# Keys and values in one transfer per block, queries in two per batch, with the heads on the same partitions

## The chip, the core and the metric

The kernel runs on one core of a Trainium2 chip. The metric is device time in microseconds (us), from the first to the last instruction of that core. The core has a matrix engine (TensorE, PE in the profile), whose weight loads are listed apart (PEld), three engines for elementwise work (VectorE, DVE; ScalarE, ACT; GpSimd, POOL) and SyncE (SP), which here only issues transfers. Transfers between the main memory and the core's own memory of 128 partitions run on 16 transfer engines; an engine that issues one spends time of its instruction queue on it (SPq, ACTq, POOLq in the profile). Engines run on their own and wait for each other by semaphores.

## The reference

A retention layer (attention with a fixed decay per head instead of a softmax), then a layer of experts with one expert for each token.

```python
# q, k, v: (8, 8, 576, 64) float32: batch, heads, positions, width of a head
scores = (1 / np.sqrt(64)) * (q @ k.transpose(0, 1, 3, 2))
gamma = 1.0 - 2.0 ** (-5.0 - np.arange(H))
ret = scores * np.where(rel >= 0, gamma[:, None, None] ** rel, 0.0)   # rel = position of q - position of k
x = (ret @ v) as rows of 4608 tokens x 512
probs = softmax(x @ w_gate)                       # 8 experts
out[token] = probs[its best expert] * (relu(x[token] @ w1[e]) @ w2[e])   # e: its best expert
```

## The kernel before

The 576 positions of a batch are cut into four blocks of 128 (`c` = 0 to 3) and a last one of 64 (`c` = 4): 40 blocks in all, numbered `i`. The decay is split into a factor on the keys (`kg`) and one on the queries (`qg`), so that the scores of a block need a triangular mask alone; what lies before the block comes in through a running state (`se`). Keys of a block are loaded (`kt`), scaled on GpSimd (`kk`), transposed on TensorE (`psk`), copied by ScalarE (`kT`), and multiplied with the transposed queries (`pssc`); VectorE masks the scores (`sc`), TensorE multiplies them with the values (`psx`), VectorE copies the result (`xT`), and it goes, transposed back (`psr`, `xr`), to rows of tokens in main memory (`x_rows`), from which the experts' stage gathers its tokens.

```python
P, B, H, S, DH = 128, 8, 8, 576, 64
NP, NCH, REM, NCOL = H // 2, 4, 64, 5
# ... `after(ins, dep)` lets `ins` go only when `dep` is done; ldk has 7 buffers per tag, ldq 2 ...
    def load_q(b, p, dep=None):

        if p == 0:
            qts[b] = ldq.tile([P, H, NCH, DH], F32, tag="q", name="qt")
        h = 2 * p
        after(nc.sync.dma_start(out=qts[b][:, h:h + 2, :, :],
                                in_=q[b, h:h + 2, 0:NCH * P, :].rearrange("h (p s) d -> p h s d", p=P)), dep)


    def load_kv(store, tag, src, i, part, dep):
        b, c = blocks[i]
        if i not in store:
            store[i] = ldk.tile([P, H, DH], F32, tag=tag, name=tag + "t")
        t = store[i]
        hs = slice(part * NP, (part + 1) * NP)
        for u in range(part + 1):
            ps = slice(0, P) if part == 0 else slice(u * REM, (u + 1) * REM)
            t0 = c * P + ((1 - u) * REM if part else 0)
            n = P if part == 0 else REM
            after(nc.sync.dma_start(out=t[ps, hs, :], in_=src[b, hs, t0:t0 + n, :].rearrange("h p d -> p h d")), dep)

    def load_k(i, part=None, dep=None):

        if i >= NB:
            return
        b, c = blocks[i]
        for u in range(2) if part is None else (part,):
            if c < NCH:
                load_kv(kts, "k", k, i, u, dep)
                continue
            if i not in kts:
                kts[i] = ldk.tile([P, H, DH], F32, tag="k", name="kt")
            after(nc.sync.dma_start(out=kts[i][u * REM:(u + 1) * REM, :, :],
                                    in_=(q, k)[u][b, :, NCH * P:S, :].rearrange("h p d -> p h d")), dep)

    def load_v(i, part=None, dep=None):

        if i >= NB:
            return
        b, c = blocks[i]
        for u in range(2) if part is None else (part,):
            if c < NCH:
                load_kv(vts, "v", v, i, u, dep)
                continue
            if i not in vts:
                vts[i] = ldk.tile([P, H, DH], F32, tag="v", name="vt")
            after(nc.sync.dma_start(out=vts[i][u * REM:(u + 1) * REM, 0:NP, :],
                                    in_=v[b, u * NP:(u + 1) * NP, NCH * P:S, :].rearrange("h p d -> p h d")), dep)

    load_k(0)
    for p in range(NP):
        load_q(0, p)
    load_v(0)
    load_k(1)
    load_v(1)
    load_q(1, 0)
    for i in range(2, 5):
        load_k(i)
        load_v(i)
        load_q(1, i - 1)
    # ... factors kg, qg; for heads 4 to 7 of a full block kg is made for the swapped halves ...
        mask = attc.tile([P, NP, P], F32, name="mask")
        nc.gpsimd.memset(mask[:, :, :], 0.0)
        for p in range(NP):
            e_ = (p // 2) * REM
            o_ = REM - e_
            nc.gpsimd.tensor_copy(out=mask[e_:e_ + REM, p, 0:REM], in_=tri[e_:e_ + REM, :])
            nc.gpsimd.memset(mask[e_:e_ + REM, p, REM:P], 1.0)
            nc.gpsimd.tensor_copy(out=mask[o_:o_ + REM, p, REM:P], in_=tri[o_:o_ + REM, :])
        return tri, mask
    # ...
    def scale_k(i):
        if i >= NB:
            return
        kk = wk3.tile([P, H, DH], F32, tag="kk")
        nc.gpsimd.tensor_tensor(out=kk[:, :, :], in0=kts.pop(i)[:, :, :],
                                in1=kg[:, blocks[i][1], :].unsqueeze(2).to_broadcast([P, H, DH]), op=ALU.mult)
        kks[i] = kk

    def stage_TK(i):
        if i >= NB:
            return
        kk = kks[i]
        pst = psw.tile([P, 512], F32, tag="W", name="psk")
        for p in range(NP):
            tr(pst[:, p * P:(p + 1) * P], kk[:, 2 * p:2 * p + 2, :].rearrange("p h d -> p (h d)"), ident[:, :])
        kT = wkp.tile([P, NP, P], F32, tag="kT")
        mark["kT"] = nc.scalar.copy(out=kT[:, :, :].rearrange("p a t -> p (a t)"), in_=pst[:, :])
        kTs[i] = kT

    def stage_SC(i):
        if i >= NB:
            return
        b, c = blocks[i]
        kT = kTs.pop(i)
        sc = wkp.tile([P, 2, NP, P], F32, tag="sc")
        scs[i] = sc
        if c < NCH:
            qT = qTs[b]
            for p in (0, 2, 1, 3):
                for o in range(2):
                    u = (p // 2) ^ o
                    for j in range(2):
                        r = slice(j * DH, (j + 1) * DH)
                        mm(pssc[u * DH:(u + 1) * DH, j, p * P + o * DH:(p + 1) * P], kT[r, p, u * DH:(u + 1) * DH],
                           qT[r, p, c * P + o * DH:(c + 1) * P], True, True)
            mark["sc"] = nc.vector.tensor_tensor(
                out=sc[:, :, :, :].rearrange("p j a i -> p j (a i)"), in0=pssc[:, :, :],
                in1=mask[:, :, :].rearrange("p a i -> p (a i)").unsqueeze(1).to_broadcast([P, 2, NP * P]),
                op=ALU.mult)
    # ... else: the last block of 64 ...
```

A matmul of the scores uses 64 of the 128 rows and 64 of the 128 columns of the array: `r` chooses the rows (head `j` of a pair), `u` the columns. Keys of the first half of a block are multiplied with all 128 queries, those of the second half with the last 64 only. Heads 0 to 3 have the first half of the keys on partitions 0 to 63; heads 4 to 7 have it on partitions 64 to 127, which is why `load_kv` loads those heads in two pieces.

The main loop, with what paces the loads (`mark`):

```python
    for i, (b, c) in enumerate(blocks):
        mark.clear()
        if i == 1:
            make_routing()
        if c < NP and b + 1 < B:
            scale_q(b + 1, c)
        scale_k(i + 3)
        stage_SC(i + 1)
        load_k(i + 6, 0, mark.get("sc"))
        stage_TK(i + 2)
        load_k(i + 6, 1, mark.get("kT"))
        stage_S(i + 1)
        load_v(i + 6, 0, mark.get("se"))
        if rf is not None:
            steps(rf, 0.6)
        if i > 0:
            stage_R(i - 1)
        if c == 0 and b > 0:
            stage_L1(b - 1)
        stage_AV(i)
        load_v(i + 6, 1, mark.get("xT"))
        if c < NP and b + 2 < B:
            load_q(b + 2, c, mark.get("xT"))
        if c < NP and b + 1 < B:
            stage_TQ(b + 1, c)
        if c == 0 and b > 0:
            stage_L2(b - 1)
        for (e, j), m in zip(early.get(i, ()), ("sc", "kT", "xT")):
            load_w(e, j, 4, wpool, mark.get(m))
        if (b, c) == (B // 2, 1):
            rf = route_first()
        if rf is not None:
            steps(rf, 0.8)
```

`stage_R` sends the rows of a full block to `x_rows` in one transfer and those of a last block in two, both issued by SyncE. Weights of the first four experts come in 32 pieces: one each in blocks 12, 16, 20, 24 and 28, three each in the last seven blocks (33 to 39), and the other six after the loop. GpSimd issues them.

Of the kernel before, what the change touches and what calls it, by code (L numbers as in the profile page):

```python
# [11 lines left out]
ALU = mybir.AluOpType  # L12
# [29 lines left out]
def kernel(  # L42
# [55 lines left out]
    def load_q(b, p, dep=None):  # L98

        if p == 0:  # L100
            qts[b] = ldq.tile([P, H, NCH, DH], F32, tag="q", name="qt")
        h = 2 * p
        after(nc.sync.dma_start(out=qts[b][:, h:h + 2, :, :],  # L103
                                in_=q[b, h:h + 2, 0:NCH * P, :].rearrange("h (p s) d -> p h s d", p=P)), dep)


    def load_kv(store, tag, src, i, part, dep):
        b, c = blocks[i]
        if i not in store:
            store[i] = ldk.tile([P, H, DH], F32, tag=tag, name=tag + "t")  # L110
        t = store[i]
        hs = slice(part * NP, (part + 1) * NP)
        for u in range(part + 1):
            ps = slice(0, P) if part == 0 else slice(u * REM, (u + 1) * REM)
            t0 = c * P + ((1 - u) * REM if part else 0)
            n = P if part == 0 else REM
            after(nc.sync.dma_start(out=t[ps, hs, :], in_=src[b, hs, t0:t0 + n, :].rearrange("h p d -> p h d")), dep)  # L117

    def load_k(i, part=None, dep=None):
# [4 lines left out]
        for u in range(2) if part is None else (part,):  # L124
            if c < NCH:
                load_kv(kts, "k", k, i, u, dep)
                continue
            if i not in kts:
                kts[i] = ldk.tile([P, H, DH], F32, tag="k", name="kt")
# [3 lines left out]
    def load_v(i, part=None, dep=None):  # L133
# [4 lines left out]
        for u in range(2) if part is None else (part,):  # L138
            if c < NCH:
                load_kv(vts, "v", v, i, u, dep)  # L140
                continue
            if i not in vts:
                vts[i] = ldk.tile([P, H, DH], F32, tag="v", name="vt")
# [4 lines left out]
    for p in range(NP):  # L148
        load_q(0, p)
# [3 lines left out]
    load_q(1, 0)  # L153
    for i in range(2, 5):
        load_k(i)
        load_v(i)
        load_q(1, i - 1)
# [9 lines left out]
    tok = attc.tile([P, 3, NCOL], F32, name="tok")  # L167
# [4 lines left out]
    for u in range(2):  # L172
# [531 lines left out]
    for i, (b, c) in enumerate(blocks):  # L704
# [20 lines left out]
        if c < NP and b + 2 < B:  # L725
            load_q(b + 2, c, mark.get("xT"))
# [242 lines left out]
```

## Time and profile before

| | before |
|---|---|
| time, median of 3 runs | 422.88 us (415.46 to 425.97) |
| span of the profiled run, granted TensorE clock | 422.9 us, 0.943 |
| busy: PE, PEld | 349.8 us (83%), 246.7 us (58%) |
| busy: DVE, ACT, POOL | 159.6 us (38%), 130.1 us (31%), 196.8 us (47%) |
| transfers issued by SyncE | 97152 packets, 33.08 MB, 32.5% of 16 engines' span |
| transfers issued by GpSimd | 18176 packets, 31.47 MB, 34.2% |
| chain that ended last | PE 58%, DMA 18%, SPq 10%, POOL 4%, others |

How to read it: the busy share is the time in which an engine has an instruction of its own under way; issuing a transfer and waiting do not count, so SyncE has no busy time at all here although its queue may be full. The chain that ended last is followed back from the last instruction, at each step to what released it: its shares say on what the end hung, engine by engine. In the attention stage, to about 240 us, one sees keys (`kt`), the queue that issues them (SPq) and TensorE in that chain; after that, TensorE and the weights. L numbers are lines of the kernel: L117 loads keys and values, L103 queries, L271 scales keys, L329 masks scores, L60 and L63 are the helpers that record all matmuls and transposes.

### The profile page before, as it was taken

How to read it: one execution, taken by the hardware profiler on the slowest of the kernel's cores; microseconds unless marked ns; L12 is line 12 of the kernel's file. 1: busy time of each engine (PE TensorE's matmuls, PEld its weight loads, DVE VectorE, ACT ScalarE, POOL GpSimd, SP SyncE). 2: the span in 40 equal slices, each digit the busy share in tenths (PEclk: the TensorE clock that was granted, in tenths of full speed). 3: DMA queues.
4: the chain of work that ended last, by engine and by line, in shares of the span. 5: the costliest groups of instructions: out<-in, count | busy, mean ns of one | idle time of the engine just before them, and what ended most of it. 6: DMA issues, size and time to landing. Idle time of an engine off the chain costs nothing.

```text
span 422.9 us, 11389 instructions
## 1 busy us (share of the span) xinstructions
PE 349.8 (83%) x4626; PEld 246.7 (58%) x4642; DVE 159.6 (38%) x360; ACT 130.1 (31%) x292; POOL 196.8 (47%) x244
## 2 busy tenths in 40 slices
PE   3698986987988878958896659968999999999970
PEld 2486765865866657646675446735555656565630
DVE  3142423341433575714475359512223333232320
ACT  3233442233242432321431222223333332323320
POOL 5752332332424433336764543765656654455320
PEclk9998998898999989969899969989999999999995
DMA  6746665576677767488799999989578822223120
GB/s 174 172 95 141 160 163 150 139 161 166 159 170 166 172 144 184 117 202 208 180 191 189 205 208 230 207 195 192 131 174 189 196 98 98 88 90 112 68 76 22
DMA packets 115389, 65.37 MB, mean 155 GB/s; under 512 B 86142, under 2 KB 107646, under 8 KB 115328
## 3 DMA queue, kind: packets, MB, share of 16 engines
q0 software_dynamic: 18176, 31.47, 34.2%
q1 hardware_dynamic: 97152, 33.08, 32.5%
q8 instruction: 39, 0.64, 0.6%
q14 instruction: 22, 0.18, 0.1%
HBM read 67.14 MB, written 15.20 MB: 195 GB/s over the span
## 4 chain that ended last, share of the span: by engine, by line
PE 58%; DMA 18%; SPq 10%; POOL 4%; issue 3%; DVE 2%; ACT 1%; another core or an unknown queue 1%; POOLq 0%; ACTq 0%
PE py L60 16%; PE pm L60 16%; DMA kt<-in_k_dram 12%; PE psx L60 7%; SPq L117 5%; DMA w2b<-in_moe_w_dram 4%; PE psk L63 4%; POOL kk L271 3%; PE pssc L60 3%; PE pss L60 3%; PE psr L63 3%; PE psq L63 2%; PE pt L63 2%; PE psl L60 1%; SPq L103 1%
## 5 line engine op out<-in xcount | busy, mean ns | idle before, releaser
L271 POOL TENSOR_TENSOR kk<-kt,kg 128x512 f32<-128x512 f32 x40 | 41.9, 1047 | 119.9 <-DMA kt<-in_k_dram 100.0
L794 ACT ACTIVATE ht<-pm 128x384 bf16<-128x384 f32 (+1 forms) x96 | 50.4, 526 | 106.7 <-PE pm L60 98.2
L60 PE MATMUL pm<-xt,w1b 128*128 128x256 bf16 (+1 forms) x512 | 74.6, 305 | 5.6 <-DVE xt L778 5.1
L60 PE MATMUL py<-w2b,ht 128*128 128x512 bf16 x304 | 71.1, 386 | 4.0 <-ACT ht L794 2.5
L809 POOL DMA_INDIRECT out_dram<-ys,tids x40 | 40.8, 1020 | 64.7 <-DVE ys L808 57.9
L60 PEld LDWEIGHTS <-w1b 128*128 128x128 bf16 x512 | 51.0, 100 | 28.6 <-issue 5.9
L63 PE MATMUL psk<-ident,kk 128*128 128x128 f32 x160 | 28.8, 307 | 38.7 <-POOL kk L271 38.6
L60 PEld LDWEIGHTS <-ht 128*128 128x128 bf16 x320 | 30.9, 99 | 39.1 <-issue 3.4
L329 DVE TENSOR_TENSOR sc<-pssc,mask 128x1024 f32<-128x1024 f32 x32 | 39.1, 1221 | 27.0 <-PE pssc L60 14.1
L808 DVE TENSOR_SCALAR ys<-py,gat 128x512 f32<-128x512 f32 x40 | 30.0, 750 | 50.8 <-PE py L60 48.8
L369 DVE COPY xT<-psx 128x512 f32<-128x512 f32 x32 | 22.1, 691 | 66.1 <-PE psx L60 61.1
L648 POOL DMA_INDIRECT xg<-x_rows,tidg x40 | 41.0, 1026 | 11.9 <-issue 9.3
L293 ACT COPY kT<-psk 128x512 f32<-128x512 f32 x40 | 23.4, 586 | 72.9 <-PE psk L63 72.5
L63 PEld LDWEIGHTS psk<-ident,kk 128*128 128x128 f32 x160 | 18.3, 150 | 43.9 <-POOL kk L271 41.7
L60 PE MATMUL psx<-sc,vt 128*64 128x128 f32 (+1 forms) x640 | 39.6, 273 | 0.0
L778 DVE COPY xt<-pt 128x512 bf16<-128x512 bf16 x40 | 15.8, 421 | 54.4 <-PE pt L63 49.4
L261 POOL TENSOR_TENSOR qq<-qt,qg 128x512 f32<-128x512 f32 x32 | 34.0, 1063 | 1.3 <-DMA qt<-in_q_dram 1.1
L60 PEld LDWEIGHTS psx<-sc,vt 128*64 128x64 f32 (+1 forms) x640 | 30.6, 138 | 6.1 <-issue 5.5
L60 PE MATMUL pssc<-qT,kT 64*64 64x128 f32 (+1 forms) x1024 | 32.2, 257 | 1.2 <-issue 0.8
L60 PEld LDWEIGHTS pssc<-qT,kT 64*64 64x64 f32 x1024 | 25.5, 138 | 8.1 <-issue 5.0
L283 ACT COPY qT<-psq 128x512 f32<-128x512 f32 x32 | 19.2, 600 | 32.2 <-PE psq L63 32.2
L310 ACT COPY se<-pss 128x256 f32<-128x256 f32 x32 | 11.9, 372 | 46.5 <-PE psx L60 36.8
(119 smaller groups left out, 361.9 us busy)
## 6 DMA issues: line engine op xcount, KB each, us to landing
qt<-in_q_dram SPq DMA_DIRECT2D x32, 256.0 KB
kt<-in_k_dram SPq DMA_DIRECT2D x40, 128.0 KB
vt<-in_v_dram SPq DMA_DIRECT2D x80, 64.0 KB
kt<-in_k_dram SPq DMA_DIRECT2D x64, 64.0 KB
vt<-in_v_dram SPq DMA_DIRECT2D x32, 128.0 KB
x_rows<-xr SPq DMA_DIRECT2D x32, 128.0 KB
w1b<-in_moe_w_dram POOLq DMA_DIRECT2D x16, 256.0 KB
w2b<-in_moe_w_dram POOLq DMA_DIRECT2D x16, 256.0 KB
```

What stands on the lines that cost most here:

```text
L60: nc.tensor.matmul(out=out, lhsT=lhsT, rhs=rhs, start=start, stop=stop, skip_group_check=True)
L63: nc.tensor.transpose(out=out, in_=in_, identity=identity)
L117: after(nc.sync.dma_start(out=t[ps, hs, :], in_=src[b, hs, t0:t0 + n, :].rearrange("h p d -> p h d")), dep)
L261: nc.gpsimd.tensor_tensor(out=qq[:, :, :].rearrange("p s (h d) -> p h s d", d=DH), in0=qts[b][:, h0:h0 + 2, :, :], in1=qg[:, 0:NCH, h0:h0 ...
L271: nc.gpsimd.tensor_tensor(out=kk[:, :, :], in0=kts.pop(i)[:, :, :], in1=kg[:, blocks[i][1], :].unsqueeze(2).to_broadcast([P, H, DH]), op=A ...
L293: mark["kT"] = nc.scalar.copy(out=kT[:, :, :].rearrange("p a t -> p (a t)"), in_=pst[:, :])
L329: mark["sc"] = nc.vector.tensor_tensor(out=sc[:, :, :, :].rearrange("p j a i -> p j (a i)"), in0=pssc[:, :, :], in1=mask[:, :, :].rearrang ...
L369: mark["xT"] = nc.vector.tensor_copy(out=xTs[b][:, c, :].rearrange("p (w t) -> p w t", w=2), in_=psx[:, :, 0:2 * P])
L648: nc.gpsimd.indirect_dma_start(out=xg[:, :], out_offset=None, in_=x_rows[0:nr, :], in_offset=bass.IndirectOffsetOnAxis(ap=slots[ph][1][:, ...
L794: nc.scalar.activation(out=ht[:, f0:f0 + per, :], in_=pm[:, :, :], func=AF.Relu)
L808: nc.vector.tensor_scalar(out=ys[:, :], in0=py[:, :], scalar1=gat[:, i:i + 1], scalar2=None, op0=ALU.mult)
L809: nc.gpsimd.indirect_dma_start(out=next(outs)[:, :], out_offset=bass.IndirectOffsetOnAxis(ap=tids[:, i:i + 1], axis=0), in_=ys[:, :], in_o ...
```

## The change

Keys and values of a full block come in one transfer each, all eight heads with their positions on the same partitions, instead of three each; the swapped halves of heads 4 to 7 are given up, and with them the third set of decay factors, the two kinds of mask and the order of the score matmuls that went with them. Queries come in two transfers of four heads per batch instead of four of two heads; those of the first batch are issued by ScalarE while SyncE issues keys and values. The pace marks are spread anew. It is for fewer issues: each transfer costs its issuing queue some time, whatever its size.

```diff
--- before.py
+++ after.py
@@ -95,66 +95,57 @@
     NB = len(blocks)
     qts, kts, vts, qrs = {}, {}, {}, {}
 
-    def load_q(b, p, dep=None):
-
-        if p == 0:
+    def load_q(b, g, dep=None, eng=None):
+
+        if g == 0:
             qts[b] = ldq.tile([P, H, NCH, DH], F32, tag="q", name="qt")
-        h = 2 * p
-        after(nc.sync.dma_start(out=qts[b][:, h:h + 2, :, :],
-                                in_=q[b, h:h + 2, 0:NCH * P, :].rearrange("h (p s) d -> p h s d", p=P)), dep)
-
-
-    def load_kv(store, tag, src, i, part, dep):
+        hs = slice(g * NP, (g + 1) * NP)
+        after((eng or nc.sync).dma_start(out=qts[b][:, hs, :, :],
+                                         in_=q[b, hs, 0:NCH * P, :].rearrange("h (p s) d -> p h s d", p=P)), dep)
+
+    def load_kv(store, tag, src, i, dep):
         b, c = blocks[i]
-        if i not in store:
-            store[i] = ldk.tile([P, H, DH], F32, tag=tag, name=tag + "t")
-        t = store[i]
-        hs = slice(part * NP, (part + 1) * NP)
-        for u in range(part + 1):
-            ps = slice(0, P) if part == 0 else slice(u * REM, (u + 1) * REM)
-            t0 = c * P + ((1 - u) * REM if part else 0)
-            n = P if part == 0 else REM
-            after(nc.sync.dma_start(out=t[ps, hs, :], in_=src[b, hs, t0:t0 + n, :].rearrange("h p d -> p h d")), dep)
-
-    def load_k(i, part=None, dep=None):
+        store[i] = ldk.tile([P, H, DH], F32, tag=tag, name=tag + "t")
+        after(nc.sync.dma_start(out=store[i][:, :, :],
+                                in_=src[b, :, c * P:(c + 1) * P, :].rearrange("h p d -> p h d")), dep)
+
+    def load_k(i, dep=None):
 
         if i >= NB:
             return
         b, c = blocks[i]
-        for u in range(2) if part is None else (part,):
-            if c < NCH:
-                load_kv(kts, "k", k, i, u, dep)
-                continue
-            if i not in kts:
-                kts[i] = ldk.tile([P, H, DH], F32, tag="k", name="kt")
+        if c < NCH:
+            load_kv(kts, "k", k, i, dep)
+            return
+        kts[i] = ldk.tile([P, H, DH], F32, tag="k", name="kt")
+        for u in range(2):
             after(nc.sync.dma_start(out=kts[i][u * REM:(u + 1) * REM, :, :],
                                     in_=(q, k)[u][b, :, NCH * P:S, :].rearrange("h p d -> p h d")), dep)
 
... load_v likewise: one transfer for a full block, two for the last block ...
     load_k(0)
-    for p in range(NP):
-        load_q(0, p)
+    load_q(0, 0, eng=nc.scalar)
+    load_q(0, 1, eng=nc.scalar)
     load_v(0)
     load_k(1)
     load_v(1)
-    load_q(1, 0)
     for i in range(2, 5):
         load_k(i)
         load_v(i)
-        load_q(1, i - 1)
+        if i < 4:
+            load_q(1, i - 2)
 
 
     lns = []
... tok, kx: the third set of decay factors goes ...
     kg = attc.tile([P, NCOL, H], F32, name="kg")
     qg = attc.tile([P, NCOL, H], F32, name="qg")
-    for j in range(2):
-        hs = slice(j * NP, (j + 1) * NP)
-        nc.vector.tensor_tensor(out=kg[:, :, hs].rearrange("p c h -> p h c"), in0=kx[:, 2 * j, 0, hs, :],
-                                in1=kx[:, 2 * j, 1, hs, :], op=ALU.mult)
+    nc.vector.tensor_tensor(out=kg[:, :, :].rearrange("p c h -> p h c"), in0=kx[:, 0, 0, :, :],
+                            in1=kx[:, 0, 1, :, :], op=ALU.mult)
     nc.vector.scalar_tensor_tensor(out=qg[:, :, :].rearrange("p c h -> p h c"), in0=kx[:, 1, 0, :, :],
                                    scalar=scale, in1=kx[:, 1, 1, :, :], op0=ALU.mult, op1=ALU.mult)
     nc.vector.tensor_copy(out=kg[0:REM, NCH, :], in_=qg[0:REM, NCH, :])
@@ -211,11 +196,9 @@
         mask = attc.tile([P, NP, P], F32, name="mask")
         nc.gpsimd.memset(mask[:, :, :], 0.0)
         for p in range(NP):
-            e_ = (p // 2) * REM
-            o_ = REM - e_
-            nc.gpsimd.tensor_copy(out=mask[e_:e_ + REM, p, 0:REM], in_=tri[e_:e_ + REM, :])
-            nc.gpsimd.memset(mask[e_:e_ + REM, p, REM:P], 1.0)
-            nc.gpsimd.tensor_copy(out=mask[o_:o_ + REM, p, REM:P], in_=tri[o_:o_ + REM, :])
+            nc.gpsimd.tensor_copy(out=mask[0:REM, p, 0:REM], in_=tri[0:REM, :])
+            nc.gpsimd.memset(mask[0:REM, p, REM:P], 1.0)
+            nc.gpsimd.tensor_copy(out=mask[REM:P, p, REM:P], in_=tri[REM:P, :])
         return tri, mask
 
 
@@ -319,13 +302,12 @@
         scs[i] = sc
         if c < NCH:
             qT = qTs[b]
-            for p in (0, 2, 1, 3):
-                for o in range(2):
-                    u = (p // 2) ^ o
+            for p in range(NP):
+                for u in range(2):
                     for j in range(2):
                         r = slice(j * DH, (j + 1) * DH)
-                        mm(pssc[u * DH:(u + 1) * DH, j, p * P + o * DH:(p + 1) * P], kT[r, p, u * DH:(u + 1) * DH],
-                           qT[r, p, c * P + o * DH:(c + 1) * P], True, True)
+                        mm(pssc[u * DH:(u + 1) * DH, j, p * P + u * DH:(p + 1) * P], kT[r, p, u * DH:(u + 1) * DH],
+                           qT[r, p, c * P + u * DH:(c + 1) * P], True, True)
             mark["sc"] = nc.vector.tensor_tensor(
                 out=sc[:, :, :, :].rearrange("p j a i -> p j (a i)"), in0=pssc[:, :, :],
                 in1=mask[:, :, :].rearrange("p a i -> p (a i)").unsqueeze(1).to_broadcast([P, 2, NP * P]),
@@ -702,18 +684,17 @@
         early[i] = [rest.pop(0) for _ in range(3)]
     rf = None
     for i, (b, c) in enumerate(blocks):
-        mark.clear()
         if i == 1:
             make_routing()
         if c < NP and b + 1 < B:
             scale_q(b + 1, c)
         scale_k(i + 3)
         stage_SC(i + 1)
-        load_k(i + 6, 0, mark.get("sc"))
+        load_k(i + 6, mark.get("sc"))
         stage_TK(i + 2)
-        load_k(i + 6, 1, mark.get("kT"))
         stage_S(i + 1)
-        load_v(i + 6, 0, mark.get("se"))
+        if c in (1, 3) and b + 2 < B:
+            load_q(b + 2, c // 2, mark.get("kT"))
         if rf is not None:
             steps(rf, 0.6)
         if i > 0:
@@ -721,9 +702,7 @@
         if c == 0 and b > 0:
             stage_L1(b - 1)
         stage_AV(i)
-        load_v(i + 6, 1, mark.get("xT"))
-        if c < NP and b + 2 < B:
-            load_q(b + 2, c, mark.get("xT"))
+        load_v(i + 6, mark.get("xT"))
         if c < NP and b + 1 < B:
             stage_TQ(b + 1, c)
         if c == 0 and b > 0:
```

## The prediction

> **What bounds the kernel now.** The kernel has two stages: attention over 40 blocks (8 batches of 5), to about 240 us, and the experts after it. I read the list of waits first, because it says which engine is late for what; then TensorE's own waits in the attention stage; then the queue of SyncE there, because every transfer of q, k and v is issued by it; last the windows, for the load of the transfers themselves.
>
> The list of waits (engine and line, what was waited for, us in total, times, longest):
>
> ```profile
> POOL kk L271 <- DMA kt<-in_k_dram: 100.0, 28, 6.5
> ...
> PE psk L63 <- POOL kk L271: 38.6, 18, 5.8
> ```
>
> GpSimd waits for keys 28 times. By itself that costs nothing, GpSimd has little to do; but TensorE in turn waits 38.6 us for the scaled keys. The same wait from 30 to 200 us, without the start and the loaded end:
>
> ```profile
> PE psk L63 <- POOL kk L271: 26.7, 15, 4.6
> ```
>
> So 26.7 us of TensorE standing still hang on keys that land late. Why late? The timeline of SyncE's queue for seven microseconds in the second batch (start, length, line, what is issued):
>
> ```profile
> 64.97 1.39 SPq L117 DMA_DIRECT2D vt<-in_v_dram  x1
> 66.45 0.56 SPq L103 DMA_DIRECT2D qt<-in_q_dram  x1
> 67.10 1.78 SPq L117 DMA_DIRECT2D kt<-in_k_dram  x3
> 68.97 0.56 SPq L117 DMA_DIRECT2D vt<-in_v_dram  x1
> 69.62 0.45 SPq L410 DMA_DIRECT2D x_rows<-xr  x1
> 70.17 1.26 SPq L117 DMA_DIRECT2D vt<-in_v_dram  x2
> 71.49 0.60 SPq L103 DMA_DIRECT2D qt<-in_q_dram  x1
> 72.19 1.77 SPq L117 DMA_DIRECT2D kt<-in_k_dram  x3
> ```
>
> One issue follows the other without a hole, some 0.6 us each. The three issues at 67.10 bring the keys of block 12. The program lets them go when the scores of block 7 are masked (L329), and the timeline of VectorE has that at
>
> ```profile
> 50.63 1.22 DVE L329 TENSOR_TENSOR sc<-pssc,mask 128x1024 f32<-128x1024 f32 x1 [0.52 <-PE pssc L60]
> ```
>
> that is, over at 51.86. The keys could have gone then, and went 15.2 us later. Over blocks 6 to 36 I find 12 to 18 us each time: about the three blocks of lead that the program gives them. The lead is eaten by the queue. The chain of waits shows what follows (start, length, what):
>
> ```profile
> 67.61 0.61 SPq L117
> 68.27 2.70 DMA kt<-in_k_dram
> 71.22 1.02 POOL kk L271
> 72.28 1.11 PE psk L63 x4
> ```
>
> Keys land 2.7 us after the last of their three issues, are scaled, and TensorE starts at once. SyncE's issues set the pace of attention. They fit it: per batch 4 for q, 4x3+2 for k, 4x3+2 for v, 4+2 for x_rows, 38 in all, by 0.65 us (0.60 and the step to the next) 24.7 us, and short waits for the paces in between; a batch takes 25.5 to 31.5 us (starts of the first xT of each batch, 23.04 to 220.91 us: 28.3 on average).
>
> The windows (columns: busy time of PE, weight load, DVE, ACT, POOL, granted clock, DMA share, GB/s):
>
> ```profile
> 37.00:200.00 163.00, 136.86 (x2591) 107.25 (x2587) 67.41 (x128) 53.95 (x135) 60.27 (x61) 0.93 0.69 163
> 200.00:254.00 54.00, 40.65 (x710) 31.66 (x711) 27.24 (x76) 16.28 (x42) 30.11 (x40) 0.91 1.03 195
> 254.00:423.00 169.00, 148.01 (x972) 88.88 (x986) 54.27 (x122) 47.97 (x92) 84.77 (x86) 0.96 0.56 135
> ```
>
> Until 200 us the transfer engines are busy 0.69, TensorE 0.84. From 200 to 254 us they are full (1.03): here the weights of the experts come in.
>
> **What the Trainium skill says.** "DMA: Bandwidth & Descriptors", section "Issuing engines are not separate DMA queues": issues from ScalarE, SyncE and GpSimd run on the same 16 transfer engines; a second issuing engine saves the issue time alone, which the page calls usually small. The trace agrees with the mechanism and not with "small": here the issue time is the bound, at 0.6 us a piece and 38 pieces a batch. "SBUF — State Buffer", section "Can I just issue two DMAs to hit both halves?": two transfers of half the partitions do not add up to one over all, and one over all 128 is the way. The trace of before can't show that alone. "TensorEngine Tiling (Array Packing)", section "Key Properties": tiles of the array work independently, and a change of tiling drains it. The trace agrees: the 16 score matmuls of 64x64 start some 7 ns apart in fours and overlap. This matters below.
>
> **The change part by part.**
>
> (a) Fewer issues. Keys and values of a full block fall from 3+3 to 1+1, queries of a batch from 4 to 2. Per batch 2 for q, 4+2 for k, 4+2 for v, 6 for x_rows: 20 instead of 38, 20 x 0.65 = 13 us. That is half of a batch, so the queue no longer falls behind; keys go when their pace mark is done, three blocks (some 14 us) ahead of use, and need 2.5 to 5 us to land. The 26.7 us of waits between 30 and 200 us should go. The bytes are the same, and so are the 256 B pieces. A batch of attention moves about 4.1 MB; at 163 GB/s over a share of 0.69 the engines could do 236 GB/s, so 17.5 us of 25: no new bound. Gain: 26.7 us.
>
> (b) The score matmuls lose their balance. Before, heads 4 to 7 have their two halves of keys swapped on the partitions, so that a 128-wide and a 64-wide matmul alternate between the two column halves of the array: each half gets 2x128 + 2x64 rows per head of a pair. After the change one half gets all four 128-wide and the other all four 64-wide. Every f32 matmul stands twice in the records (32 for 16), so the fuller tile streams 2x512 = 1024 rows instead of 2x384 = 768. What a row costs is read from a block without waits:
>
> ```profile
> 107.37 0.90 PE L60 MATMUL pssc<-qT,kT 64*64 64x128 f32 x32
> 108.20 0.66 PE L63 MATMUL psk<-ident,kk 128*128 128x128 f32 x4
> 108.79 0.69 PE L60 MATMUL pss<-vt,kk 128*64 128x64 f32 x16
> 109.40 0.66 PE L63 MATMUL psr<-ident,xT 128*128 128x128 f32 x4
> 109.99 1.09 PE L60 MATMUL psx<-sc,vt 128*64 128x128 f32 x16
> 111.02 0.67 PE L60 MATMUL psx<-qT,se 64*64 64x128 f32 x16
> ```
>
> From start to next start: pss has 512 rows in each column half and takes 0.61 us; the first psx has 1024 and takes 1.03. So 0.82 ns a row and 0.19 us besides; 768 rows give 0.82, and pssc takes 0.83. With 1024 it will take 1.03: 0.2 us more, on an engine that will then be the bound. Before the weights flood (27 full blocks up to block 32): 27 x 0.2 = 5.4 us lost.
>
> (c) The start. ScalarE issues q of batch 0 in two pieces at the same time as SyncE issues k. Keys of block 0 now share the engines with 1 MB of queries; GpSimd needs k, then q by halves, then builds masks, and it had waited only 2.4 us for the keys and 1 us for queries. I expect the first xT between 22.5 and 24 us, from 23.04: 0.5 us lost. ScalarE's two issues push its table load and the decay factors back by 1.3 us, to about 4.4 us, which is when the keys land. The small operations removed (iota, a negation, half of a product) take some 0.5 us beside the first transfer.
>
> (d) The end of attention. From block 33 on the paces let 21 pieces of weights go, three a block, and six more follow; the transfers are full. This stage starts earlier by whatever attention gained before, and its own length (from xT of block 33 at 212.4 to the first second-layer matmul at 254.5, 42 us) is set by bytes, which do not change. I count it as shifted, with no gain of its own. The expert stage is shifted likewise.
>
> Sum: -26.7 + 5.4 + 0.5 = -20.8 us, so 402. TensorE becomes the bound at about 25.3 us a batch (24.5 now without these waits, by the differences of xT starts less the gaps, plus 4 x 0.2). I don't expect all to come: when 15 waits go, shorter ones for other things come forward (eight gathers that hold GpSimd about 1.3 us each from 195 to 207 us, ScalarE copies, a clock that falls to half for 3.4 us about every 30 us and may do so more often when TensorE is denser). I take 4 us off the gain: 406.
>
> **Rivals.** (1) Transfers become the wait: the same bytes in less time, queries in 512 KB pieces that keys queue behind. For it: share 0.69, landing takes up to 5.1 us after the issue near 160 and 180 us. Against: 14 us of lead. If so, a third of the waits stays, about 412. (2) The lost balance outweighs: if TensorE were already the bound and the waits only filled slack, the time would be 422.9 + 6 = 429. Against: the waits are gaps of TensorE itself, with nothing else in them. (3) The weights decide: the loads of the first four experts end when their bytes have moved, and attention waits there. Then little of the gain survives, about 418. Against: they are paced by attention's own blocks, and until 200 us the engines are a third idle. (4) Better than my sum: with the backlog gone, keys and values of blocks 37 to 39 no longer compete with the weights (the last keys took 12.4 us to land), which makes (d) some 2 to 5 us shorter: 399.
>
> **Range and chances.** Rivals (1) and (3) give 412 to 418, (4) 399; the three times of before alone spread over 415 to 426. I put 8 in 10 on 397 to 415. Faster by over 2% means under 414.4: 0.82. Within 2%: 0.14. Slower needs (2) in full: 0.04.
>
> **What would show it.** Right: keys issued within some 2 us of their mark instead of 15; holes in SyncE's queue; TensorE's waits for scaled keys from 30 to 200 us under 8 us; score groups at 1.03 us instead of 0.83; batches about 25 to 26 us apart; 42 us from block 33 to the second layer. Wrong: keys that still land late though issued early (rival 1), a second-layer start that stays near 254 (rival 3), or a score group still at 0.83 us, in which case (b) is wrong and the time falls toward 400.

## The result, and the profile after

| | before | after |
|---|---|---|
| time, median (range) | 420.4 us (415.46 to 425.97, 4 runs) | 383.14 us (380.58 to 384.44, 4 runs) |
| ratio, with its 95% interval | | 0.919 [0.909, 0.929] |
| profiled span, granted TensorE clock | 422.9 us, 0.943 | 382.2 us, 0.966 |
| first xT / xT of block 33 / first matmul of the experts' second layer | 23.04 / 212.42 / 254.1 us | 26.33 / 179.72 / 218.9 us |

The change brought 37 us, over twice the 17 us that I foresaw. The last row says where. From the first xT to block 33 the kernel before took 189.4 us, the kernel after 153.4: 36.0 us less. The start lost 3.3 us, the stretch from block 33 to the second layer gained 2.5, and what follows gained 5.5. So the question is almost wholly the stretch from 25 to 210 us, where I expected 26.7 - 5.4 = 21.3 us and 36.0 came.

The wait for keys is gone. This is all that the list of TensorE's waits holds for the kernel after from 30 to 200 us (what waited, for what: us in total, times, longest):

```profile
PE psl L63 <- DVE lt L412: 1.6, 2, 0.9
PE psl L60 <- DVE rk L531: 1.4, 1, 1.4
PE psr L63 <- DVE xT L351: 0.6, 1, 0.6
```

Not one of the three is a key. SyncE's queue (start, length, line, what is issued), in the fourth batch, has holes, as from 94.92 to 96.98 us and from 97.97 to 100.09:

```profile
92.28 1.77 SPq L398 DMA_DIRECT2D x_rows<-xr  x2
94.55 0.37 SPq L109 DMA_DIRECT2D vt<-in_v_dram  x1
96.98 0.37 SPq L109 DMA_DIRECT2D kt<-in_k_dram  x1
97.45 0.52 SPq L103 DMA_DIRECT2D qt<-in_q_dram  x1
100.09 0.34 SPq L392 DMA_DIRECT2D x_rows<-xr  x1
```

And keys now go with their mark. VectorE's timeline has the masked scores of a block at 50.54, so they are over at 51.76; the next line of SyncE's queue for keys stands 0.06 us behind that, where the kernel before needed 15.2 us:

```profile
50.54 1.22 DVE L311 TENSOR_TENSOR sc<-pssc,mask 128x1024 f32<-128x1024 f32 x1 [0.71 <-PE pssc L60]
```
```profile
51.82 0.40 SPq L109 DMA_DIRECT2D kt<-in_k_dram  x1
```

The chain of waits (start, length, what) passes from transfer, scaling and matmul to TensorE alone, and shows what one group of score matmuls costs now:

```profile
52.25 1.62 PE psx L60 x32
53.87 0.59 PE psq L63 x4
54.45 1.02 PE pssc L60 x24
55.47 0.59 PE psk L63 x4
56.06 0.61 PE pss L60 x16
```

1.02 us for a pssc: term (b), foreseen at 1.03. What I did not foresee stands in the windows (stretch, length, busy PE, PEld, DVE, ACT, POOL, granted clock, DMA share, GB/s):

```profile
37.00:200.00 163.00, 159.34 (x3177) 126.57 (x3175) 93.45 (x179) 67.51 (x171) 79.78 (x84) 1.00 0.83 193
200.00:222.00 22.00, 14.41 (x174) 9.91 (x171) 10.69 (x38) 4.39 (x11) 9.39 (x15) 0.84 1.18 214
222.00:382.00 160.00, 143.81 (x971) 87.28 (x969) 51.25 (x113) 48.16 (x92) 84.81 (x86) 0.97 0.56 138
```

TensorE is busy 98% of the first stretch, and its clock is 1.00; it was 0.93. The row of the granted clock in 40 slices of the span, before and then after, shows it at a glance:

```profile
PEclk9998998898999989969899969989999999999995
```
```profile
PEclk9769999999999999999999699999999999999995
```

A slice of before is 10.6 us long, and an 8 or a 6 in it is a stretch of 3.4 or 6.8 us at half clock. From 30 to 210 us six of these stand in the trace of before, 27.2 us in all (at 36.8, 71.0, 101.7, 156.3, 183.6 and 200.7 us). If half the work is done at half clock, they cost 27.2 / 2 = 13.6 us, an estimate. From 25.5 to 209.8 us the kernel after has none. The busy time of TensorE from first xT to block 33 bears the estimate out (columns as above; before, then after):

```profile
23.04:212.42 189.38, 159.73 (x2956) 125.05 (x2957) 76.68 (x145) 63.88 (x159) 75.81 (x81) 0.93 0.67 159
```
```profile
26.33:179.72 153.39, 151.16 (x2959) 119.69 (x2959) 80.25 (x145) 63.91 (x159) 72.89 (x73) 1.00 0.81 195
```

TensorE's idle time falls from 29.65 to 2.23 us. Its busy time falls too, by 8.57 us for the same matmuls, though the score matmuls have become dearer by 5.1 us (27 blocks at 1.02 us in place of 0.83). Together that is 13.7 us of faster clock.

Each stretch follows a gap. One of them in the windows of before, cut into pieces of 3.41 us (busy time of PE, granted clock, DMA share, GB/s):

```profile
98.28:101.69 3.41, 0.96 (x35) 1.00 0.49 123
101.69:105.10 3.41, 3.41 (x46) 0.50 0.73 178
105.10:108.51 3.41, 3.41 (x81) 1.00 0.50 117
```

In the first, TensorE stood idle for 2.45 us, waiting for keys. The next runs at 0.50 though it is full of work; then the clock is back. The stretches begin on a grid of 3.41 us. Of the windows of before that were idle for 1.83 us or more (1.83, 1.87, 2.01, 2.45, 2.76) all had a window at half clock behind them; of those with 1.16, 1.26, 1.33, 1.52 and 1.55 us, only the one with 1.33.

The Trainium skill has this, in "TensorE: Matmul & The Clock Gate", section "HAM oscillation — how this bites in real kernels": waits for transfers drop TensorE to half rate, and the work after them starts slow. The prediction did not use that page. The trace agrees with the mechanism and the length of the window, but the page speaks of gaps longer than some 3.4 us, and here 1.8 us of idle time in one window were enough.

So theory A: late keys cost twice, once as a gap and once as the half clock behind it; 26.7 - 5.1 + 13.6 = 35.2 us of the 36.0. Against it stand the rivals that fewer or larger transfers are better in themselves, that the form of the transfers (partitions, heads) does it, or that the clock follows something other than the gaps, such as load or time. What each says of a run is in the expectations.

### The profile page after: what moved, and what is told of

Same layout as the page of the kernel before. It is cut to its first block, busy times and chain, and to the rows that moved or that the text cites. A ratio compares the mean times of both kernels' runs of the same rounds, so it can differ in the third digit from the quotient of the medians.

```text
span 382.2 us, 11126 instructions
## 1 busy us (share of the span) xinstructions
PE 342.5 (90%) x4642; PEld 243.2 (64%) x4642; DVE 165.3 (43%) x358; ACT 130.3 (34%) x292; POOL 197.4 (52%) x241
## 4 chain that ended last, share of the span: by engine, by line
PE 84%; DVE 5%; DMA 4%; POOL 2%; issue 1%; ACT 1%; POOLq 0%; DVEq 0%
PE pm L60 19%; PE py L60 18%; PE psx L60 13%; PE pssc L60 9%; PE psk L63 6%; PE pss L60 5%; PE psr L63 5%; PE psq L63 4%; DMA w1b<-in_moe_w_dram 2%; PE pt L63 2%; PE psl L60 1%; DMA kt<-in_k_dram 1%; DVE xt L757 1%; DVE pay L576 1%; PE pspl L60 1%
## 5 line engine op out<-in xcount | busy, mean ns | idle before, releaser
L60 PEld LDWEIGHTS <-w1b 128*128 128x128 bf16 x512 | 51.0, 100 | 28.3 <-DMA w1b<-in_moe_w_dram 5.0
L311 DVE TENSOR_TENSOR sc<-pssc,mask 128x1024 f32<-128x1024 f32 x32 | 39.1, 1221 | 29.0 <-PE pssc L60 15.3
L276 ACT COPY kT<-psk 128x512 f32<-128x512 f32 x40 | 23.4, 586 | 48.8 <-PE psk L63 48.0
L60 PE MATMUL psx<-sc,vt 128*64 128x128 f32 (+1 forms) x640 | 39.2, 270 | 0.0
L63 PE MATMUL psk<-ident,kk 128*128 128x128 f32 x160 | 27.6, 298 | 11.4 <-POOL kk L254 11.4
L60 PE MATMUL pssc<-qT,kT 64*64 64x64 f32 (+1 forms) x1024 | 37.0, 262 | 0.5 <-ACT se L293 0.5
L60 PEld LDWEIGHTS pssc<-qT,kT 64*64 64x64 f32 x1024 | 28.7, 137 | 5.7 <-issue 3.1
L232 POOL DMA_DIRECT2D w1b<-in_moe_w_dram x24 | 15.2, 639 | 27.8 <-DVE sc L311 14.9
```

What stands on the lines that cost most here:

```text
L60: nc.tensor.matmul(out=out, lhsT=lhsT, rhs=rhs, start=start, stop=stop, skip_group_check=True)
L63: nc.tensor.transpose(out=out, in_=in_, identity=identity)
L311: mark["sc"] = nc.vector.tensor_tensor(out=sc[:, :, :, :].rearrange("p j a i -> p j (a i)"), in0=pssc[:, :, :], in1=mask[:, :, :].rearrang ...
```

## The experiments

All are edits of the kernel after unless said. Times are medians; the interval is that of the ratio to the kernel before on the same chip. The kernels of this part ran on three chips; a time is set against the 383.14 us of the kernel after, which was not run again on two of them.

**Three transfers again, nothing swapped.** Only the number of issues goes back, to 36 a batch; the layout of the kernel after stays.

```diff
-        after(nc.sync.dma_start(out=store[i][:, :, :], ...), dep)
+        for hs, p0, n in ((slice(0, NP), 0, P), (slice(NP, H), 0, REM), (slice(NP, H), REM, REM)):
+            after(nc.sync.dma_start(out=t[p0:p0 + n, hs, :], ...), dep)
```

> The kernel after the change, but keys and values of a full block again in three transfers each (heads 0 to 3 over all partitions, heads 4 to 7 in two pieces of 64 partitions), nothing swapped: 36 issues per batch instead of 20. Theory A (SyncE's queue was the bound, and TensorE's waits also cost clock): the queue is full again, 36 x 0.65 = 23.4 us and short waits against 22.6 us of TensorE; keys go 8 us or more behind their mark, TensorE waits 20 us or more for scaled keys, half-clock stretches come back in the attention stage, time 405 to 425 us. Theory B (the bound was how fast the pieces move, or the layout of the score matmuls, not the number of issues): less than half of the 37 us comes back, under 400 us.

Measured: 415.46 us (414.58 to 418.81), 0.985 [0.975, 0.995]. 32 of the 37 us are gone. SyncE's queue is without holes again, and TensorE waits for keys from 30 to 200 us:

```profile
69.85 1.85 SPq L110 DMA_DIRECT2D kt<-in_k_dram  x3
71.80 0.55 SPq L393 DMA_DIRECT2D x_rows<-xr  x1
72.45 1.93 SPq L110 DMA_DIRECT2D vt<-in_v_dram  x2
```
```profile
PE psk L63 <- POOL kk L255: 16.7, 10, 2.7
```

Half clock is back too, at 123.4, 178.0 and 201.9 us, and keys go 7 to 17 us behind their mark. From first xT to block 33 this kernel takes 25.4 us more than the kernel after: 16.7 of them are waits for keys (20 or more were expected), and half of the 10.2 us at half clock are 5.1. The trace also has waits of 5.7 us at 187 and 195 us whose releaser the profile doesn't name; more of such waits below. 36 issues of 0.65 us are 23.4 us, more than the 22.58 us that a batch of the kernel after takes, so the queue falls behind, and batches grow from 22.4 to 30.5 us. The 0.65 us are too low once the queue is full: in the third batch 37 issues take 27.47 us, 0.74 us each, and in the kernel before 270 issues take 197.9 us, 0.73 each.

**Two transfers**, once as halves of the partitions with all heads, once as four heads over all partitions: 28 issues a batch.

```diff
+        for u in range(2):                    # halves
+            ps = slice(u * REM, (u + 1) * REM)
+            ... out=t[ps, :, :]
+        for g in range(2):                    # four heads, all partitions
+            hs = slice(g * NP, (g + 1) * NP)
+            ... out=t[:, hs, :]
```

> The kernel after the change, but keys and values of a full block in two transfers each, each over 64 partitions with all heads: 28 issues per batch, 18.2 us of 22.6. Theory A (number of issues): the queue still has holes, keys go within 2 us of their mark, the time stays within 1% of 383 us. Theory B (transfers over half of the partitions are the slow part): keys land late, time 395 us or more. A third view, that every issue has its price whatever the load: 8 more a batch x 0.65 x 8 batches = 42 us, so 410 to 425 us.

> The changed kernel with keys and values of a full block in two transfers each of four heads over all 128 partitions: 28 issues a batch, as in the kernel with halves of the partitions. If the 12 us that the halves cost came from the number of issues: 392 us or more here too. If from the transfers over 64 partitions: within 1% of 383 us.

Measured: 395.65 us, 0.938 [0.928, 0.947], and 397.18 us, 0.934 [0.926, 0.942]. 28 x 0.65 = 18.2 us fit into a batch, and the first four batches take 22.36 to 22.6 us in both, as in the kernel after. So in these batches the 8 issues more cost nothing, and half the partitions are no dearer than all of them. The halves are near the limit, though: their queue has hardly a hole in batches two to four (26 to 28 issues in 22.58 us, over 0.8 us each) and their keys go up to 5 us behind their mark, against 2 in the expectation; with four heads the queue has holes, and keys are 3.3 us behind at most. Both kernels still end 12 to 14 us later, and the expected 1% was missed: the halves lose 2.5 us at the start, 4 in blocks 25 to 33 and 5 in the expert stage; the other loses at 156 to 184 us and in the expert stage. By the total alone, as the second expectation put it, the number of issues would be to blame. But the losses don't stand where keys are loaded late: in the expert stage of both, and at 164 us in the second, ScalarE or VectorE stand still for 1 to 4 us behind a releaser that the profile doesn't name, with half clock after it. What costs the halves 4 us in blocks 25 to 33 is not shown: TensorE's matmuls have holes of 0.2 to 0.6 us there that the profile puts down to no wait. I come back to this below.

**Gaps put in.** Does the clock follow gaps? 26 small products on GpSimd (13.9 us) hold back the scaled keys of blocks 6, 11, 16 and 21, in the kernel that has no gaps of its own; in a second kernel TensorE transposes the identity 36 times in the place of the gap (into an unused part of the bank of the running state, which this disturbs, so that what it computes is no longer the layer; the rest of its work is the same); in a third, 20 products give shorter gaps, in blocks 6, 11 and 16.

```diff
+        if i in GAPS:
+            for _ in range(26):        # 20 in the third
+                nc.gpsimd.tensor_tensor(out=junk[:, :], in0=mask[:, 0, :], in1=mask[:, 1, :], op=ALU.mult)
         scale_k(i + 3)
 ...
+        if i - 1 in GAPS:              # the second kernel only
+            for _ in range(36):
+                tr(pss[:, 384:512], ident[:, :], ident[:, :])
```

> The kernel after the change, with 26 small extra operations on GpSimd before the scaling of keys in four blocks (6, 11, 16, 21), so that TensorE stands still for about 2 to 5 us at four places where it has no gap now; no transfer is touched. Theory A (a gap of over half of a 3.4 us window is followed by half clock): each of the four gaps is followed by a half-clock stretch of 3.4 us or more, and the time grows by the sum of the gaps and about 1.7 us or more for each: with gaps of 3 us, 12 + 7 = 19 us. Rival C (the clock falls by itself or with load, not with gaps): the time grows by the gaps alone, and no new half-clock stretch stands behind them.

> As the kernel with four gaps, but TensorE transposes a constant 36 times (some 4 us) into an unused part of a bank at the place of each gap, so that it is held up as long but not idle. Theory A: no half-clock stretch behind the four places, and the time grows by the four hold-ups alone (4 x about 4 us = 16 us or less); less than the kernel with gaps if the gaps there are as long. Rival C: the same clock as the kernel with gaps.

> As the kernel with gaps, with 20 extra operations instead of 26 and in three blocks (6, 11, 16): gaps of about 1.2 us each. Theory A with its threshold (over half of a 3.4 us window): no half-clock stretch behind them; time 3.5 to 5 us over the changed kernel. If any gap costs clock: 3 x 1.7 us more, 9 us or more over it.

The first gap on TensorE's timeline, with gap (start, length, line, matmuls; in brackets the idle time before them and who ended it):

```profile
52.22 1.09 PE L60 MATMUL pssc<-qT,kT 64*64 64x128 f32 x32
57.79 0.66 PE L63 MATMUL psk<-ident,kk 128*128 128x128 f32 x4 [4.48 <-POOL kk L254]
58.38 1.12 PE L60 MATMUL pss<-vt,kk 128*64 128x64 f32 x16
59.43 1.12 PE L63 MATMUL psr<-ident,xT 128*128 128x128 f32 x4
```

and filled:

```profile
53.32 4.15 PE L63 MATMUL pss<-ident 128*128 128x128 f32 x36
57.91 0.66 PE L63 MATMUL psk<-ident,kk 128*128 128x128 f32 x4 [0.44 <-POOL kk L254]
58.49 0.69 PE L60 MATMUL pss<-vt,kk 128*64 128x64 f32 x16
59.11 0.66 PE L63 MATMUL psr<-ident,xT 128*128 128x128 f32 x4
```

The keys come at the same time, 57.8 and 57.9 us. Behind the gap the same pss takes 1.12 us and psr 1.12; behind the filling 0.69 and 0.66. The windows of those 3.4 us (busy PE, clock, DMA share, GB/s) say the same, 34 records against 57; with gap:

```profile
54.91:58.32 3.41, 0.53 (x4) 1.00 0.60 138
58.32:61.73 3.41, 3.41 (x34) 0.50 0.02 5
```

filled:

```profile
58.00:61.40 3.40, 3.40 (x57) 1.00 0.01 1
```

| | gaps | filled | short gaps |
|---|---|---|---|
| idle time at the first three | 4.48, 4.44, 4.33 us | 0.44, 0.38, 0.40 us | 1.26, 1.24, 1.24 us |
| half clock behind them | 3.4, 6.8, 3.4 us | none | none |
| batch, over 22.58 us | +6.05, +7.33, +5.89 | +4.58, +4.53, +4.54 | +1.33, +1.30, +1.31 |
| time | 423.13 us | 414.89 us | 400.05 us |

A gap of 4.4 us costs 5.9 to 7.3: itself, and 1.6 to 2.9 us more, 0.42 to 0.46 of the stretch behind it. A delay of the same length that TensorE spends working costs only itself, and a gap of 1.25 us costs 1.3. That is theory A, and it speaks against a clock that follows load or time: only the gap is different. The fourth place, block 21, keeps a gap of 3.64 us in the filled kernel, and has half clock behind it again. The totals say less: all three are higher than expected, by 40, 32 and 17 us over the kernel after where about 19, at most 16 and 3.5 to 5 were expected, and the 17 us of the short gaps alone would speak for a price of every gap. They hold more than these batches. The short gaps add 3.9 us to the three batches; the rest comes at 160 to 185 us and at 255 us, with the unnamed waits.

**The kernel before, traced once more,** unchanged.

> The kernel before once more, for a second trace. Theory A: the half-clock stretches stand elsewhere than in the first trace, but again each begins after a 3.4 us window in which TensorE was idle for over half. Rival C: they stand at the same places or with no relation to idle time. ScalarE's wait of 2.3 us near 280 us, whose releaser the profile does not name, may be there or not: if not, it is chance and no part of the kernel.

Measured: 430.74 us, with this trace, and 423.25 us. Half clock at 74.0, 101.3, 121.8, 142.2, 159.3, 186.6, 203.7 and 231.0 us, partly at other places than in the first trace. Windows idle for 1.82 us or more had one behind them, those up to 1.42 us none, but for one of 1.48. The places move with the gaps.

**The start.** In the kernel after, TensorE's timeline at the start has this (same columns as above):

```profile
10.55 1.81 PE L63 MATMUL psq<-ident,qq 128*128 128x128 f32 x8 [0.23 <-POOL qq L244]
16.56 1.11 PE L63 MATMUL psk<-ident,kk 128*128 128x128 f32 x4 [4.20 <-POOL kk L254]
17.60 1.97 PE L60 MATMUL pssc<-qT,kT 64*64 64x128 f32 x32
```

GpSimd builds the masks from 11.46 to 15.4 us, between the queries and the second block's keys. TensorE waits 4.20 us, and the scores behind take 1.97 us in place of 1.09: half clock from 15.3 to 25.5 us. In the kernel before it is much the same there (a gap of 3.64 us, full clock from 19.8 us). The masks need no input, and can be built while the first keys are on their way:

```diff
+    tri, mask = make_masks()
     scale_k(0)
 ...
     scale_q(0, 3)
-    tri, mask = make_masks()
     scale_k(1)
```

> The changed kernel with the masks built on GpSimd before the first scaling of keys, where GpSimd waits for the first transfer anyway, instead of between the queries and the second keys. Theory A (the start costs 4.2 us of gap of TensorE behind the masks, and the half clock that follows it): the gap at 12.4 us shrinks to under 1.5 us, TensorE is at full clock several us earlier than at 25.5 us, first xT 4 to 7 us earlier, time 4 to 7 us less. Rival: the second keys have not landed either at that time (transfers are full at the start), the gap stays, under 1.5 us gained.

> The changed kernel once more, beside the next three on the same chip. 0.919 of the time before, within the interval of the first measurement. In its profile: no half-clock stretch between about 30 us and the end of attention, first xT near 26 us, 22.6 us a batch.

Measured on one chip: 377.89 us (376.92 to 378.77), 0.892 [0.887, 0.897], against 382.38 us (381.42 to 382.7), 0.902 [0.897, 0.908], for the kernel after. 4.5 us less for one line moved, the fastest of all kernels here. The same place in its timeline:

```profile
11.48 0.66 PE L63 MATMUL psq<-ident,qq 128*128 128x128 f32 x4 [0.36 <-POOL qq L244]
12.47 0.66 PE L63 MATMUL psk<-ident,kk 128*128 128x128 f32 x4 [0.34 <-POOL kk L254]
13.06 1.09 PE L60 MATMUL pssc<-qT,kT 64*64 64x128 f32 x32
```

The first xT comes at 18.88 us, 5.4 earlier than in the kernel after on that chip (24.26); 4.0 us of this is the gap, which is 4.31 us there and 0.34 here, and there is no half clock behind it.

**The first queries back on SyncE.**

```diff
-    load_q(0, 0, eng=nc.scalar)
-    load_q(0, 1, eng=nc.scalar)
+    load_q(0, 0)
+    load_q(0, 1)
```

> The changed kernel with the first queries issued by SyncE after the first keys, as before, instead of by ScalarE. If ScalarE's issues are what makes the first keys late (they share the transfers with 1 MB of queries): first scaling of keys at about 4.7 us instead of 6.1, first xT 1 us or more earlier. If they help: queries 1 us later, the time 1 us more. Either way within 1% of the changed kernel.

Measured: 394.65 us (393.82 to 395.32), 0.928 [0.921, 0.936]; the expected 1% is missed. The start itself is no worse: keys are first scaled at 3.89 us (6.07 after), the first xT comes at 23.45 us (26.33 and 24.26 in the two traces of after), and up to block 28 it stays 2.9 us ahead of the first of these. Then it loses 8 us at 153 to 185 us and 6 in the expert stage. The timeline of ScalarE has the largest of these waits, over 6 us and with no name:

```profile
166.70 0.59 ACT L266 COPY qT<-psq 128x512 f32<-128x512 f32 x1 [6.16 <-remote]
```

**Balance back.** Swapped halves and balanced score matmuls as before, three transfers for k and v, those of v from block 5 on issued by ScalarE so that neither queue overflows; and the same with the masks first.

```diff
+        eng = nc.scalar if tag == "v" and i > 4 else nc.sync
+        for hs, p0, t0, n in ((slice(0, NP), 0, 0, P), (slice(NP, H), 0, REM, REM), (slice(NP, H), REM, 0, REM)):
+            after(eng.dma_start(out=t[p0:p0 + n, hs, :], in_=src[b, hs, c * P + t0:c * P + t0 + n, :] ...), dep)
```

> The changed kernel with the swapped halves of heads 4 to 7 and the balanced order of the score matmuls of the kernel before; keys and values need three transfers each again, and from block 5 on those of the values are issued by ScalarE, so that SyncE has 22 issues a batch and ScalarE 14. If the unbalanced score matmuls cost 0.2 us a block on the path: a group takes 0.83 us instead of 1.02, a batch 21.8 us instead of 22.6, time 5 to 7 us less. Rival: ScalarE's issues (14 x 0.65 = 9 us a batch beside 8 us of its own work) hold up its copies, and the gain is lost or turned round, time the same or up to 10 us more.

> Both of the last two together. If they add: 9 to 14 us less than the changed kernel, 370 to 376 us where that one has 383. If ScalarE becomes the bound: no better than the kernel with the masks first.

Measured: 408.44 us, 0.966 [0.959, 0.973], and 408.71 us, 0.963 [0.957, 0.969]. The score group is back at 0.83 us, and yet 26 us are lost against the kernel after on that chip, where the rival view gave up to 10. TensorE's waits name the new bound:

```profile
PE psr L63 <- ACT xr L402: 17.6, 14, 3.1
```

ScalarE issues in line with its own copies, and while it issues, the copies (`xr`) that TensorE waits for don't run. Between 30 and 150 us this makes four gaps of 2.2 to 3.1 us. Half clock follows two of them (at 92.2 and 119.5 us), but not the gaps of 2.34 and 2.17 us at 36 and 148 us, whose idle time falls into two windows each; a third stretch, at 163.8 us, follows a wait for VectorE. Moving the masks gains nothing on top of this.

## Why the prediction was wrong, point by point

Its mechanism held: the queue of SyncE was the bound, and lifting it removed the waits. The time lies outside the range because one term was missing, and two were mis-sized. From the 402 us of its sum, before the margin:

| | foreseen | measured | difference |
|---|---|---|---|
| (a) waits for keys gone | -26.7 | -26.7 | 0 |
| half clock behind these waits gone | 0 (more of it, in the margin) | -13.6 | -13.6 |
| (b) score matmuls out of balance | +5.4 | +5.1 | -0.3 |
| rest of the stretch from first xT to block 33 | 0 | -0.8 | -0.8 |
| (c) start | +0.5 | +3.3 | +2.8 |
| (d) block 33 to second layer | 0 | -2.5 | -2.5 |
| expert stage | 0 | -5.5 | -5.5 |

Sum: 402.1 - 19.9 = 382.2 us, the profiled run.

- **(a)** Right in each sign that it named: issues with their mark, holes, and no wait for keys where "under 8 us" was the test. Three issues again bring them back. The price of an issue was set too low, 0.65 us where the full queue takes 0.73; so 38 of them alone make the 28.3 us of a batch, with no need of the "short waits for the paces in between".
- **(b)** Right: 1.02 us, and 0.83 when the balance is put back. The score matmuls start 7 ns apart in pairs, though, and not "in fours".
- **The step that failed** is the clock, in the sum and then in the margin: "a clock that falls to half for 3.4 us about every 30 us and may do so more often when TensorE is denser". It is the reverse. The clock fell because TensorE was not dense, and it stopped falling when the gaps went. I had read the stretches as a property of time. What stands ahead of each is a window with 1.3 to 2.8 us of idle time, and the inserted and filled gaps show that idle time is the cause. The same step hid in "24.5 now without these waits", the time of a batch: this took away the gaps and left their shadow in. (28.27 us - (26.7 + 13.6) / 7 = 22.5, plus 0.8 for (b): 23.3 us; the mean of the seven is 23.18.) And the 4 us of margin went the wrong way.
- **(c)** Mis-sized. The keys are first scaled at 6.07 us in place of 4.71: of this delay, 1.4 us, I had let 0.5 through to the first xT, and 1.2 came through. The other 2 us of the 3.3 are the half clock behind the gap at the masks. It lasts to 25.5 us in this trace and to 20.8 in the second of the same kernel, whose first xT comes at 24.26 us (1.2 over before): the two traces differ in where the gap falls on the clock's grid.
- **(d)** 2.5 us less, in the range that rival (4) gave. Its reason, fewer transfers beside the weights, was not tested, and the two traces of the kernel before differ by more than that in this stretch (41.7 and 46.1 us).
- **The expert stage**, "shifted likewise", lost a wait of ScalarE and the half clock behind it. In ScalarE's timeline of before, and in the windows of PE there:

```profile
281.47 1.09 ACT L794 ACTIVATE ht<-pm 128x512 bf16<-128x512 f32 x2 [2.27 <-remote]
```
```profile
279.20:282.60 3.40, 0.87 (x3) 1.00 0.67 172
282.60:286.00 3.40, 3.40 (x10) 0.50 1.07 165
```

A wait of 2.27 us and half of 3.4 make 4 of the 5.5 us. Neither trace of after has it. Why not stays open.
- **Rivals (1) to (3)** fell: keys need 4.7 us from issue to landing (median) with 14 us of lead; the waits were gaps, and worth more than their length; the second layer starts at 218.9 us, not near 254. Two signs named for "right" failed with the clock: batches are 22.4 to 25.6 us apart, not 25 to 26, and it takes 39.2 us, not 42, from block 33 to the second layer.

Shown: that the clock halves behind gaps which leave TensorE idle for 1.8 us or more of one window, that the count of issues makes these gaps (three transfers and the halves, on one chip, differ from the second batch on), and that the masks make the one at the start. Argued from the traces alone: the split of the 36.0 us, as no run keeps the gaps and has the full clock. Open: the unnamed waits, and with them most of why the kernels with two transfers and the one with SyncE's queries lie 11 to 14 us above the kernel after though their batches keep pace up to 150 us.

## What to carry to other kernels

Where TensorE is the bound, count a wait of 2 us or more as its own length and, if it falls into one 3.4 us window, some 0.4 to 0.5 of a 3.4 us stretch besides, and look at the granted clock behind each gap before you call half clock a given. Count issues: number per batch times the price of one (0.73 us in a full queue here) has to stay below the batch's time on the engine that bounds it; well below that, 20 issues in place of 28 made no batch up to 116 us faster. Setup work that needs no input belongs ahead of the first wait, where it fills a hole in place of making one.

## What the runs showed that I had not expected

- The clock falls behind short gaps: a window of 3.41 us of which 1.8 us and more were idle was always followed by half clock in both traces of the kernel before, 1.25 us was not in the test of short gaps. In between it is not sharp: 1.33 and 1.48 us did it once each, 1.52 and 1.55 us did not, and neither did a window of 1.81 us (at 34 us in the kernel with the balance back).
- An issue mostly takes 0.4 to 0.6 us on SyncE, but some at the start of the kernel after take far more; why was not tested:

```profile
5.89 2.67 SPq L109 DMA_DIRECT2D kt<-in_k_dram  x1
12.62 2.83 SPq L103 DMA_DIRECT2D qt<-in_q_dram  x1
```

- ScalarE and VectorE can stand still for 1 to 6 us behind a releaser that the profile calls "remote". The semaphore in question is always TensorE's, so it is TensorE's word that comes late. In the kernel with SyncE's queries ScalarE waits until 166.70 us for transposes (`psq`) which TensorE's timeline ends at 162.81; TensorE's semaphore moves at 163.67 and not again before 166.62 us. TensorE has idle time there for which the profile knows no wait ("issue"):

```profile
162.15 0.66 PE L63 MATMUL psq<-ident,qq 128*128 128x128 f32 x4
164.20 0.41 PE L63 MATMUL psl<-ident,lt 128*128 128x128 f32 x2 [1.39 <-issue]
```

What holds TensorE up is open. The waits before 205 us fall together with two groups of four gathers on GpSimd (from 160.8 and 170.5 us in this kernel), but the kernel after has these gathers too, from 163.7 and 171.0 us, and no such wait. Neither are small edits shown to be the reason: all eight traces of two of the three chips have such waits, also the kernel before in its second trace (three, where the first has one), and none of the four traces of the third chip has one. The kernel after was not run on those two chips, so edit and chip are not told apart, and the 11 to 14 us above may in part be the chip's.
